# Eight raw first slots instead of seven, the eighth expert's weights read twice, and a new order

## The chip, the cores and the metric

The kernel runs on one core of a Trainium2 chip. The core has a matrix array (PE), a vector engine (DVE), an activation engine (ACT), GpSimd (POOL) and an engine that issues transfers (SP). ACT and GpSimd issue transfers too. The metric is the device time of one execution in microseconds. The time before is the median of three runs, 1015.27 us (1010.53 to 1015.96).

## The reference

A gated scan over 4 sequences of 5056 tokens with 256 features, and then a mixture of 8 experts of which each of the 20224 tokens takes the one with the highest logit:

```python
log_a = c * sig_r * np.log(np.clip(a_base, 1e-06, 1.0 - 1e-06))[None, None, :]
a_t = np.exp(log_a)
norm = np.sqrt(np.maximum(1.0 - a_t * a_t, 1e-06))
x_gated = norm * sig_i * x
for t in range(S):
    h = a_t[:, t] * h + x_gated[:, t]
    y[:, t] = h
...
logits = x @ w_gate                  # x is y, tokens by 256
e_idx = np.argmax(logits, axis=1)    # and gate_w, its softmax weight
eom = 1.0 / (1.0 + np.exp(-(x @ w_output_gate)))
for e in range(E):
    mask = e_idx == e
    h = np.maximum(x[mask] @ w1[e], 0.0)     # 256 x 1024
    ye = h @ w2[e]                           # 1024 x 256
    out[mask] = gate_w[mask, None] * eom[mask, e, None] * ye
```

Here sig_r, sig_i and a_base are sigmoids of r_gate, i_gate and a_param, and c is 8.

## The kernel before

**Chunks.** The 158 tiles of 128 tokens are taken in 21 chunks: two of 4 tiles, eighteen of 8, one of 6. A chunk's features lie on the partitions, in blocks of 512 tokens. For each chunk SP loads r, i and x (L659). ACT computes the gates by two tanh passes (L665, L668), the decay and its square by exponentials (L675, L679) and a square root (L684); the root and the exponential need different function tables, and each change of table is an instruction of its own. DVE forms the products (L671, L687) and scans along the tokens (L719). ACT and DVE then cut the state into a high and a low half precision part (L879, L886); between the parts lie 128 columns of zeros per tile, the pads, set by DVE at L884. A transposing DMA on SP's queue (L895) turns it into rows of tokens, and PE forms the logits (L903).

**Routing.** DVE finds each token's expert (`choose`, `chosen`), PE counts the token's rank among those of the same expert with a matmul against a triangle and, for each tile, one against ones (`ranks`, L960 and L962, nine matmuls for eight tiles), DVE turns the ranks to positions, the scale and the token's number (`weights`, L978 to L987). GpSimd writes each tile's rows to these positions in a store in DRAM (`xs`, L456, an indirect DMA).

**Slots.** A slot is up to 128 (later 256) rows of one expert. After the chunks 1, 3, 4, 5, 6, 8 and more, a set of eight slots follows, one for each expert (`SETS`): slots 0 to 7 belong to chunk 1, 8 to 15 to chunk 3, 16 to 23 to chunk 4. The last 19 and a loop for the rest choose their expert on the chip. A slot fetches its rows by a transposing DMA on SP (L1135), PE multiplies with w1 (tile ph), ACT takes the positive part (h, L1228 or L1232), DVE the low half of it (L1235), PE multiplies with w2 (po), ACT scales (ot, L1303), and GpSimd writes the rows to the output (L1306).

**Weights.** There are 16 units, w1 and w2 of each expert, 1 MB each. A unit is loaded in single precision (L512), PE forms a gram of it (pg, L538) from which a scale follows, and ACT (L580) and DVE (L590) cut it into two half precision parts. A split slot takes three products of such parts: 48 matmuls in layer 1 (L1207) and 24 in layer 2 (L1282). A plain slot multiplies with the raw weights in single precision (L1193, L1268), 16 matmuls in each layer, which the profile shows as 32 and 16 records. Plain are the slots 0 to 6. Expert 7's slot is split; its weights are staged in the ring `hh` (tiles fw). The raw unit u lies where the parts of unit u+2 will lie, so those can't be written until the slots that read the raw ones are done (`used_raw`).

**Order.** `in_order` (L120) is a planner written by hand: each piece of work has an engine, a cost, what it comes after, and a rank from tables (`UNIT_RANK`, `CHUNK_RANK`, `SLOT_RANK`, ...). It sets the order of PE, ACT and DVE. The DMA issues on SP and ACT's queue and GpSimd's work follow one another in the order in which the planner emits them (`queue`, L302). The load of unit u waits until that of unit u - 4 has landed (`DEPTH`). The store `xs` is first filled with rows of zeros, by two transfers (`fill`, tile zrow).

## Time and profile before

| | before |
|---|---|
| median of 3 runs | 1015.27 us |
| range | 1010.53 to 1015.96 us |
| profiled execution | 1015.02 us |
| its span | 1013.3 us |
| mean granted clock of PE | 0.986 |
| PE busy | 941.1 us (93%) |
| DVE busy | 681.7 us (67%) |
| ACT busy | 618.0 us (61%) |
| POOL busy | 345.6 us (34%) |

The span runs from the first to the last instruction; the profiled execution's time has 1.7 us around it. Busy times are unions over an engine's instructions. Times in views are counted from the start of the span. In a view an arrow with a name behind an instruction is what ended the idle time ahead of it.

### The profile page before, as it was taken

To read this page: it belongs to the slowest core of one execution; us is meant where nothing else is said; L and a number is where in the kernel's file an instruction comes from. 1 tells how busy PE (TensorE), PEld (TensorE's weight loads), DVE (VectorE), ACT (ScalarE), POOL (GpSimd) and SP (SyncE) were. 2 spreads that over 40 slices of the span, in tenths; PEclk is the share of its full clock that TensorE was granted. 3 is DMA by queue.
4 is the path that set the end of the run, shared out by engine and by line. 5 is a ranking of instruction groups with operands and counts; after the bars stand their busy time and mean duration, and the time that the engine had idled before them with its cause. 6 is when DMAs were issued, how large, how long until landed. Compare 5 with 4: busy or idle time off the path is not lost.

```text
span 1013.3 us, 27790 instructions
## 1 busy us (share of the span) xinstructions
PE 941.1 (93%) x10820; PEld 862.8 (85%) x10820; DVE 681.7 (67%) x1718; ACT 618.0 (61%) x929; POOL 345.6 (34%) x339
## 2 busy tenths in 40 slices
PE   1389958999999999999999999999999999999996
PEld 1279947999999899998888888888888888899996
DVE  5779999988988798888888888786222222222321
ACT  8779998886776777686768787732322223223332
POOL 1202353344445444444344434453211212121111
PEclk9989978999999999999999999999999999999999
DMA  9999678999999999999988798667212222137771
GB/s 332 388 315 236 175 226 213 217 195 204 216 248 192 241 213 234 189 226 224 226 208 218 198 233 218 141 132 222 58 53 53 53 54 44 46 110 250 225 229 44
DMA packets 269703, 189.96 MB, mean 187 GB/s; under 512 B 211548, under 2 KB 222558, under 8 KB 269568
## 3 DMA queue, kind: packets, MB, share of 16 engines
q1 hardware_dynamic: 249904, 138.57, 59.4%
q0 software_dynamic: 15456, 42.22, 13.2%
q10 hardware_dynamic: 4208, 7.34, 2.0%
q8 instruction: 88, 1.44, 0.6%
q14 instruction: 47, 0.39, 0.1%
HBM read 79.09 MB, written 45.02 MB: 122 GB/s over the span
## 4 chain that ended last, share of the span: by engine, by line
PE 64%; issue 13%; DMA 8%; DVE 6%; ACT 5%; POOL 3%; SPq 0%; POOLq 0%; ACTq 0%; DVEq 0%
PE ph L1207 29%; PE po L1282 28%; DMA xt<-xs 3%; DMA it<-in_i_gate_dram 2%; POOL out_dram L1306 2%; PE ph L1193 2%; DMA w1r<-in_moe_w_dram 2%; DMA rt<-in_r_gate_dram 1%; DVE h L1235 1%; PE lg L903 1%; DVE it L719 1%; PE pg L538 1%; PE po L1268 1%; DVE peak L771 1%; DMA out_dram<-ot,osc 1%
## 5 line engine op out<-in xcount | busy, mean ns | idle before, releaser
L1282 PE MATMUL po<-w2r,h 128*128 128x256 f16 (+1 forms) x3744 | 517.6, 273 | 3.7 <-DVE w2r L590 1.8
L1207 PE MATMUL ph<-xt,w1r 128*128 128x128 f16 (+1 forms) x4656 | 454.3, 242 | 10.0 <-DVE h L1235 3.2
L1207 PEld LDWEIGHTS <-w1r 128*128 128x128 f16 x4656 | 362.7, 98 | 40.0 <-issue 4.2
L1282 PEld LDWEIGHTS <-h 128*128 128x128 f16 x3744 | 346.1, 98 | 40.1 <-issue 5.7
L1235 DVE SCALAR_TENSOR_TENSOR h<-ph,h 128x512 f16<-128x512 f32 x312 | 206.4, 684 | 231.9 <-ACT h L1232 227.8
L1306 POOL DMA_INDIRECT out_dram<-ot,osc x163 | 167.8, 1030 | 397.9 <-ACT ot L1303 349.7
L1232 ACT ACTIVATE h<-ph 128x512 f16<-128x512 f32 x312 | 177.7, 592 | 193.8 <-PE po L1282 175.1
L456 POOL DMA_INDIRECT xs<-rows_all,posi x158 | 174.2, 1103 | 255.9 <-ACT h L1232 87.9
L1303 ACT ACTIVATE ot<-po,osc 128x256 f32<-128x256 f32 x163 | 72.3, 469 | 126.7 <-PE po L1282 63.6
L719 DVE TENSOR_TENSOR_SCAN it<-rt,last,it 128x512 f32<-128x512 f32 (+4 forms) x78 | 94.6, 1238 | 0.3
L1207 PE MATMUL ph<-xt,ws 128*128 128x128 f16 x912 | 69.5, 219 | 0.0
L1207 PEld LDWEIGHTS <-ws 128*128 128x128 f16 x912 | 60.5, 98 | 2.6
L687 DVE SCALAR_TENSOR_TENSOR it<-it,xt 128x1024 f32<-128x1024 f32 (+1 forms) x40 | 48.3, 1207 | 20.7 <-ACT it L684 20.7
L675 ACT ACTIVATE rt<-rt,lam 128x512 f32<-128x512 f32 (+1 forms) x80 | 61.2, 802 | 0.5
L886 DVE SCALAR_TENSOR_TENSOR rt<-it,scale,rt 128x512 f16<-128x512 f32 (+1 forms) x76 | 50.3, 702 | 11.8 <-ACT rt L879 11.5
L671 DVE SCALAR_TENSOR_TENSOR xt<-it,xt 128x1024 f32<-128x1024 f32 (+1 forms) x40 | 48.3, 1208 | 7.5 <-ACT it L668 7.4
L668 ACT ACTIVATE it<-it 128x1024 f32<-128x1024 f32 (+1 forms) x40 | 41.7, 1043 | 11.4 <-DMA it<-in_i_gate_dram 8.0
L665 ACT ACTIVATE rt<-rt 128x1024 f32<-128x1024 f32 (+1 forms) x40 | 41.8, 1044 | 10.0 <-DMA rt<-in_r_gate_dram 7.9
L679 ACT ACTIVATE it<-rt 128x1024 f32<-128x1024 f32 (+1 forms) x40 | 41.8, 1044 | 6.7 <-DVE xt L671 4.6
L684 ACT ACTIVATE it<-it,quarter 128x1024 f32<-128x1024 f32 (+1 forms) x40 | 45.1, 1135 | 0.3
L879 ACT ACTIVATE rt<-it,scale 128x1024 f16<-128x1024 f32 (+1 forms) x38 | 41.1, 1131 | 5.8 <-DVE scale L793 5.7
L771 DVE TENSOR_REDUCE peak<-it 128x1 f32<-128x1024 f32 (+1 forms) x34 | 39.5, 1195 | 0.0
(181 smaller groups left out, 674.3 us busy)
## 6 DMA issues: line engine op xcount, KB each, us to landing
rt<-in_r_gate_dram SPq DMA_DIRECT2D x39, 512.0 KB
it<-in_i_gate_dram SPq DMA_DIRECT2D x39, 512.0 KB
xt<-in_x_dram SPq DMA_DIRECT2D x39, 512.0 KB
ws<-w1r SPq DMA_DIRECT2D x38, 512.0 KB
w1r<-in_moe_w_dram ACTq DMA_DIRECT2D x4, 1024.0 KB
w2r<-in_moe_w_dram SPq DMA_DIRECT2D x4, 1024.0 KB
w2r<-in_moe_w_dram ACTq DMA_DIRECT2D x3, 1024.0 KB
w1r<-in_moe_w_dram SPq DMA_DIRECT2D x3, 1024.0 KB
```

Source lines behind the costliest of these rows:

```text
L456: op = nc.gpsimd.indirect_dma_start(out=xs[:, :], out_offset=bass.IndirectOffsetOnAxis(ap=pos, axis=0), in_=rows.bitcast(F32), in_offset=None,
L671: nc.vector.scalar_tensor_tensor(t("xt"), t("it"), 1.0, t("xt"), op0=ALU.add, op1=ALU.mult)
L675: nc.scalar.activation(r[:, h], r[:, h], AF.Exp, scale=lam[:, h:h + 1], bias=lam[:, h:h + 1])
L719: nc.vector.tensor_tensor_scan(H[:, h, lo:hi], A[:, h, lo:hi], H[:, h, lo:hi], first, op0=ALU.mult, op1=ALU.add)
L771: nc.vector.tensor_reduce(tiles["peak", c][:, b // 4:b // 4 + 1], tiles["it", key][:, :, 0:m], axis=AX.XY, op=ALU.max, apply_absolute_valu ...
L886: nc.vector.scalar_tensor_tensor(halves(key, 1, m // P)[:, :, h], of_tiles(key, m)[:, :, h], tiles["scale_of", c], halves(key, 0, m // P)[ ...
L1207: nc.tensor.matmul(ph[:, i, 0:w], lhsT=ws[:, f // 2 % 2, a, c, f % 2 * P:(f % 2 + 1) * P], rhs=xt[:, b * ND + c, 0:w], start=k == 0, stop= ...
L1232: newest["relu"] = nc.scalar.activation(part(0, f0), tiles["ph", s, f0][:, :, 0:w], AF.Relu).ins
L1235: nc.vector.scalar_tensor_tensor(part(1, f0), tiles["ph", s, f0][:, :, 0:w], 0.0, part(0, f0), op0=ALU.max, op1=ALU.subtract)
L1282: nc.tensor.matmul(po[0:pw, j], lhsT=hh[:, a, f % 4, j * P:j * P + pw], rhs=second(b), start=f + j + a + b == 0, stop=f == NF - 1 and a == ...
L1303: nc.scalar.activation(ot[0:pw], tiles["po", s][0:pw, j], AF.Copy, scale=tiles["osc", s][0:pw, j, 0:1])
L1306: op = nc.gpsimd.indirect_dma_start(out=out[:, :], out_offset=bass.IndirectOffsetOnAxis(ap=tiles["osc", s][0:pw, j, 1:2].bitcast(I32), axi ...
```

## The change

Expert 7 becomes the first in turn, and its raw weights take the places of expert 0's parts (`at = (u + 2) % 16`). All eight first slots are plain, and so are the second slots of experts 5 and 6 (`AGAIN`, slots 13 and 14). So expert 7's parts are cut later, from a second load in the ring `hh`, ahead of slot 19 (`RETURN`), and slot 15, its second one, follows slot 18. The logarithm in the decay, an activation before, is now a series on DVE alone. The pads are set by GpSimd, in its queue, and wait for the block's scan; the transposing DMA waits for them. GpSimd writes the tokens' numbers too. From chunk 8 on (`SUMS`) the ranks take three matmuls and a short scan on DVE in place of nine matmuls. Sums take one reduction for two, the weights one step fewer, and the last state is copied only at a chunk's end. The tables of ranks are new.

The diff, cut to its core:

```diff
-UNIT_RANK = (120.607, 156.984, -22.135, ...
+UNIT_RANK = (209.083, 164.775, 223.789, ...
-RAWS = 7
-LAST = 7
+AGAIN = (5, 6)
+RETURN = 19
+SUMS = 8
...
+    def size_of():
+        nc.vector.scalar_tensor_tensor(ab_, ap, -1.0, ap, op0=ALU.mult, op1=ALU.min)
+        nc.vector.tensor_scalar(lo, ap, 0.0, None, op0=ALU.min)
     def exp_of():
-        nc.scalar.activation(ab_, ap, AF.Exp, scale=-1.0)
+        nc.scalar.activation(ab_, ab_, AF.Exp)
-    def ln_of():
-        nc.scalar.activation(lo, ab_, AF.Ln)
...
-    def unit(u, staged):
+    def load_unit(u):
+        at = (u + 2) % len(units)
+        fw = place_of(at).bitcast(F32)
...
+            if at >= DEPTH:
+                tc.add_manual_dep(
+                    ins.ins, tiles["load", at - DEPTH].name,
...
+    def split_unit(u, staged=None):
...
+            read.append(work("SP", DMA_ISSUE, load, [old], UNIT_LOAD[u + 2], dma=2.6 / g, uses=[use], share=0.5 if i else 2.0))
...
+        def pads(key, m):
+            a = plane(key, 2, 0, 0)
+            queue("Pool", nc.gpsimd.memset(bass.AP(a.tensor, a.offset, [a.ap[0], [PITCH, m // P - 1], [1, P]]), 0.0))
         def rest_of(key, m):
-            if m > P:
-                a = plane(key, 2, 0, 0)
-                nc.vector.memset(bass.AP(a.tensor, a.offset, [a.ap[0], [PITCH, m // P - 1], [1, P]]), 0.0)
...
+                pw = [work("Pool", 0.4, lambda key=key, m=m: pads(key, m), [states[b // 4]], late_rank, uses=[pl])] if m > P else []
-                    work("SP", 0.85 + 1.45 * scale, lambda b=b, key=key, m=m: flip(b, key, m), [hw, lw] + olds, ...
+                    work("SP", 0.85 + 1.45 * scale, lambda b=b, key=key, m=m: flip(b, key, m), [hw, lw] + pw + olds, ...
...
+            if c >= SUMS:
+                up = tiles["up", c][:, 0:E * nt].rearrange("p (e j) -> p j e", e=E)
+                to = pk[:, 0:nt * E].rearrange("p (j e) -> p j e", e=E)
+                nc.tensor.matmul(to, lhsT=not_after, rhs=st("oh", E), start=True, stop=False, skip_group_check=True)
+                nc.tensor.matmul(to, lhsT=ones16, rhs=up, start=False, stop=False, skip_group_check=True)
+                nc.tensor.matmul(pk[:, nt * E:(nt + 1) * E], lhsT=ones16, rhs=up[:, nt - 1], start=False, stop=True, skip_group_check=True)
+                return
...
+        def numbers():
+            cuts = cuts_of(row_at, nt)
+            for b, e in zip(cuts[:-1], cuts[1:]):
+                mi = rows_all[:, row_at[b]:row_at[b] + e - b, META + 2:META + 4].bitcast(I32)
+                queue("Pool", nc.gpsimd.iota(mi, pattern=[[P, e - b], [0, 1]], base=(t0 + b) * P, channel_multiplier=1))
...
-        plain = expert is not None and c == min(SETS) and expert < RAWS
+        plain = expert is not None and (c == first_set or c == second_set and expert in AGAIN)
...
+    turn = [E - 1] + list(range(E - 1))
...
+        if c == first_set:
+            for e in turn[:AHEAD]:
                 weights_of(e)
+            for k, e in enumerate(turn):
+                if k + AHEAD < E:
+                    weights_of(turn[k + AHEAD])
+                slot(slots_in[c][e])
+            continue
         for s in slots_in[c]:
-            if s < n_full:
+            if s == RETURN:
+                for u in (2 * E - 2, 2 * E - 1):
+                    split_unit(u, STAGED[u])
+                slot(2 * E - 1)
+            if s < n_full and s != 2 * E - 1:
                 slot(s)
```

What moves stands in the order of the instructions. SP's queue, from the loads of the fourth chunk (names end in the chunk's number, its first tile and a serial number) to the first fetch; xt16_0 and xt16_7 are the rows of slot 0 and slot 7, xs the store, w1r and w2r the weights. Before:

```order
L659 DMA rt_3_4_282<-in_r_gate_dram 128x2x512
L512 DMA w2r_132<-in_moe_w2_dram 128x8x256
L512 DMA w1r_131<-in_moe_w1_dram 128x2x1024
L659 DMA it_3_0_363<-in_i_gate_dram 128x2x512
L512 DMA w2r_132<-in_moe_w2_dram 128x8x256
L659 DMA xt_3_4_451<-in_x_dram 128x2x512
L512 DMA w2r_132<-in_moe_w2_dram 128x8x256
L659 DMA xt_4_0_482<-in_x_dram 128x2x512
L512 DMA w1r_131<-in_moe_w1_dram 128x2x1024
L1124 TENSOR_LOAD firsti_1_416
L1135 ISA
L1135 DMA_TRANSPOSE xt16_0_567<-xs_84 128x4x128
```

After:

```order
L680 DMA rt_3_4_282<-in_r_gate_dram 128x2x512
L680 DMA it_2_4_309<-in_i_gate_dram 128x2x512
L504 DMA w1r_142<-in_moe_w1_dram 128x2x1024
L680 DMA it_3_0_408<-in_i_gate_dram 128x2x512
L504 DMA w2r_143<-in_moe_w2_dram 128x8x256
L504 DMA w1r_142<-in_moe_w1_dram 128x2x1024
L504 DMA w2r_143<-in_moe_w2_dram 128x8x256
L680 DMA xt_3_4_484<-in_x_dram 128x2x512
L680 DMA xt_4_0_512<-in_x_dram 128x2x512
L1178 TENSOR_LOAD firsti_1_469
L1189 ISA
L1189 DMA_TRANSPOSE xt16_7_517<-xs_84 128x4x128
```

The first fetch is one of expert 7 and follows loads of chunks 3 and 4; before, it followed a load of weights. The two fills of `xs` that stood apart (the second before chunk 11) are both issued ahead of the first fetch: the second stands one row ahead of the piece shown.

ACT's instructions where the split slots begin, up to the first relu of a split slot (h_7_0 before, h_8_0 after); dg is the square of a gram, ot a slot's result, fw14 the two staged halves of expert 7's w1, w1r and w2r the weights. Before:

```order
L544 ACTIVATE dg_14_1481,sq_14_1482<-pg_14_1455 128x128
L668 ACTIVATE it_5_0_1262<-it_5_0_1262 128x1024
L665 ACTIVATE rt_5_4_1389<-rt_5_4_1389 128x1024
L580 ACTIVATE w1r_131<-fw14_0_1401,wsc_133 128x4x256
L580 ACTIVATE w1r_131<-fw14_1_1421,wsc_133 128x4x256
L580 ACTIVATE w2r_132<-w2r_132,wsc_133 128x2048
L879 ACTIVATE rt_4_0_907<-it_4_0_741,scale_4_1499 128x4x256
L879 ACTIVATE rt_4_4_998<-it_4_4_1201,scale_4_1499 128x4x256
L675 ACTIVATE rt_5_0_1327<-rt_5_0_1327,lam_94 128x512 x2
L679 ACTIVATE it_5_0_1262<-rt_5_0_1327 128x1024
L1232 ACTIVATE h_7_0_1569<-ph_7_0_1512 128x4x128
```

After:

```order
L1357 ACTIVATE ot_3_0_1509<-po_3_1463,osc_3_1269 128x256
L1282 ACTIVATE h_6_1518<-ph_6_0_1372 128x512
L1282 ACTIVATE h_6_1518<-ph_6_4_1437 128x512
L598 ACTIVATE w1r_142<-w1r_142,wsc_144 128x4x256
L1357 ACTIVATE ot_4_0_1533<-po_4_1491,osc_4_1331 128x256
L598 ACTIVATE w1r_142<-w1r_142,wsc_144 128x4x256
L598 ACTIVATE w2r_143<-w2r_143,wsc_144 128x2048
L1357 ACTIVATE ot_5_0_1606<-po_5_1520,osc_5_1427 128x256
L1286 ACTIVATE h_8_0_1620<-ph_8_0_1567 128x4x128
L1286 ACTIVATE h_8_1_1666<-ph_8_4_1613 128x4x128
```

Before, the split slot 7 starts behind both staged halves of expert 7's w1, the split of a w2, two high parts of chunk 4 and chunk 5's decay. Now slot 8 is the first split slot; plain slots' relus and results and the splits of other experts' weights stand ahead of it, and no staged weights.

GpSimd's queue around the scatters of chunk 3 (posi_3). Before:

```order
L1306 DMA out_0_dram<-ot_4_0_1403,osc_4_1149 20224x256
L456 DMA xs_84<-rows_all_130,posi_3_1360 172032x264
L1306 DMA out_0_dram<-ot_5_0_1438,osc_5_1323 20224x256
L456 DMA xs_84<-rows_all_130,posi_3_1360 172032x264
L1306 DMA out_0_dram<-ot_6_0_1453,osc_6_1423 20224x256
L456 DMA xs_84<-rows_all_130,posi_3_1360 172032x264 x6
L456 DMA xs_84<-rows_all_130,posi_4_1729 172032x264
```

After:

```order
L921 MEMSET rt_4_0_979 128x3x128
L1042 IOTA rows_all_141 128x8
L461 DMA xs_84<-rows_all_141,posi_3_1213 172032x264 x5
L921 MEMSET rt_4_4_1016 128x3x128
L461 DMA xs_84<-rows_all_141,posi_3_1213 172032x264 x3
L1360 DMA out_0_dram<-ot_2_0_1381,osc_2_1112 20224x256
L1360 DMA out_0_dram<-ot_3_0_1509,osc_3_1269 20224x256
L1360 DMA out_0_dram<-ot_4_0_1533,osc_4_1331 20224x256
L1360 DMA out_0_dram<-ot_5_0_1606,osc_5_1427 20224x256
L1360 DMA out_0_dram<-ot_6_0_1749,osc_6_1633 20224x256
```

The pads of chunk 4's two blocks (rt_4_0, rt_4_4) and the row of numbers now stand ahead of and among the scatters of chunk 3.

## Rows read from the trace of the kernel before

**Rows 1.** The page, part 1: busy us, share of the span, instructions.

```profile
PE 941.1 (93%) x10820; PEld 862.8 (85%) x10820; DVE 681.7 (67%) x1718; ACT 618.0 (61%) x929; POOL 345.6 (34%) x339
```

**Rows 2.** Busy us by stretch: length, engines, PEclk, DMA share, GB/s.

```profile
0.00:71.80 71.80, 29.59 (x255) 26.59 (x255) 49.68 (x159) 54.64 (x76) 12.03 (x26) 0.95 1.04 356
71.80:131.90 60.10, 60.06 (x514) 55.69 (x515) 55.56 (x122) 57.62 (x79) 16.40 (x15) 1.00 0.86 213
131.90:162.00 30.10, 16.48 (x190) 13.00 (x189) 28.28 (x62) 29.48 (x36) 13.99 (x10) 0.72 0.72 188
162.00:300.00 138.00, 135.30 (x1941) 127.55 (x1939) 123.04 (x299) 107.57 (x154) 61.53 (x57) 1.00 0.99 218
```

**Rows 3.** Timeline of PE: start us, us, work, count [idle before <-releaser].

```profile
62.16 1.09 PE L538 MATMUL pg<-w1r 128*128 128x128 bf16 x16 [1.95 <-DMA w1r<-in_moe_w_dram]
...
71.77 2.50 PE L1193 MATMUL ph<-xt,w1r 128*128 128x128 f32 x20 [0.37 <-DVE xt L1177]
```

**Rows 4.** Timelines of ACT's and SP's DMA queues (ACTq, SPq).

```profile
52.11 0.39 ACTq L512 DMA_DIRECT2D w1r<-in_moe_w_dram  x1
...
62.13 0.39 SPq L512 DMA_DIRECT2D w1r<-in_moe_w_dram  x1
63.48 1.31 SPq L1135 DMA_TRANSPOSE xt<-xs  x1
```

**Rows 5.** Timeline of ACT: first plain relu, first relu of slot 8.

```profile
74.56 0.58 ACT L1228 ACTIVATE h<-ph 128x512 f32<-128x512 f32 x1
...
161.96 0.58 ACT L1232 ACTIVATE h<-ph 128x512 f16<-128x512 f32 x1
```

**Rows 6.** Groups of ACT, 74.5 to 162: count, busy us, mean ns, idle.

```profile
L580 ACT ACTIVATE w1r<-w1r,wsc 128x1024 f16<-128x1024 f32 x12 | 13.1, 1138 | 0.5 <-PE ph L1193 0.5
L580 ACT ACTIVATE w2r<-w2r,wsc 128x2048 f16<-128x2048 f32 x6 | 12.0, 1992 | 0.0
...
L684 ACT ACT_TABLE_LOAD x5 | 6.4, 1283 | 0.1
L668 ACT ACTIVATE it<-it 128x1024 f32<-128x1024 f32 x6 | 6.3, 1047 | 0.5 <-DMA it<-in_i_gate_dram 0.5
```

**Rows 7.** Chain that ended last, 0 to 330: start us, us, PE's pieces.

```profile
93.05 1.35 PE po L1268 x6
...
95.14 5.02 PE ph L1193 x44
...
205.48 1.97 PE po L1282 x18
...
265.41 1.68 PE ph L1207 x30
```

**Rows 8.** A group of PE, 71.7 to 162: rank matmuls.

```profile
L962 PE MATMUL pk<-oh,ones 128*128 128x64 f16 (+7 forms) x24 | 1.1, 187 | 0.0
```

**Rows 9.** Groups of DVE, 74.5 to 162: the lower halves of the splits.

```profile
L590 DVE SCALAR_TENSOR_TENSOR w1r<-w1r,wsc 128x1024 f16<-128x1024 f32 x12 | 15.0, 1279 | 0.3 <-ACT w1r L580 0.3
L590 DVE SCALAR_TENSOR_TENSOR w2r<-w2r,wsc 128x2048 f16<-128x2048 f32 x6 | 14.1, 2345 | 0.0
```

**Rows 10.** DMA issues by tile: xcount, KB each.

```profile
xs<-zrow SPq DMA_DIRECT2D x2, 1056.0 KB
```

**Rows 11.** DVE's pads and POOL's scatters over the span; one scatter.

```profile
L884 DVE MEMSET rt<- 128x192 uint32 x37 | 8.1, 218 | 0.0
...
L456 POOL DMA_INDIRECT xs<-rows_all,posi x158 | 174.2, 1103 | 255.9 <-ACT h L1232 87.9
...
147.56 2.51 POOL L456 DMA_INDIRECT xs<-rows_all,posi  x1 [2.57 <-ACT h L1232]
```

**Rows 12.** Waits of PE over the span: us in total, times, longest us.

```profile
PE prow L839 <- DVE last L722: 20.1, 1, 20.1
...
PE ph L1207 <- DVE h L1235: 3.2, 5, 1.0
...
PE ph L1207 <- DMA xt<-xs: 1.7, 3, 1.0
```

263 lines of the change are left out of this document (142 added, 121 removed).

## The prediction

> **What bounds the kernel now.** I read the page's first part, then busy time by stretch, and only then single waits. The page says that the array (PE) is busy 93% of the span [rows 1]. The stretches say that the missing 7% lie in two places at the front [rows 2]: to 71.8 us PE works 29.59 us, and from 131.9 to 162 us 16.48 of 30.10. Between them it is full (60.06 of 60.10), after them nearly (135.30 of 138, and no great gap later). So a microsecond is won where PE is idle in front, or where PE's work shrinks.
>
> The first gap ends with the first plain matmul at 71.77 [rows 3]. Ahead of it PE waits for the weights of unit 4, whose gram starts at 62.16; totals, logits and three more grams follow. The queue views tell why so late [rows 4]: ACT's queue issues unit 4 at 52.11 only, and SP, waiting for that transfer before its own weight load, issues this at 62.13 and the first fetch of routed rows (on the same queue) at 63.48.
>
> The second gap is ACT's. From the first plain relu at 74.56 to slot 8's first relu at 161.96 [rows 5] lie 87.4 us, and rows 2 show ACT busy 57.62 of 60.10 and 29.48 of 30.10 there: 96 to 98%. DVE is below that in the first of the two (55.56). PE is done with the seven plain slots at 131.9 and waits, since ACT (gates of the coming chunk, weight splits, table loads [rows 6]) hands over the split weights late. So that stretch lasts as long as ACT's list of work, and what leaves that list shortens it one for one, until DVE is as long.
>
> **The change part by part.**
>
> *Start (order).* The SP order now has the fetch for expert 7 right behind the loads, not behind a load that waits for unit 4. PE still needs a gram of the unit that ACT's queue issues last, so the landing at 62.2 stays; what follows it before the first plain matmul is one gram (1.1), totals (0.6), logits and another gram, 4 to 5 us where 9.6 lay [rows 3]. I take 67, against 71.8. Bounds: 62, if that unit's load leaves the queue earlier, and 72, if nothing moves. The order also puts the second fill of the routed store (xs<-zrow, 1056 KB [rows 10]) into the loads at the start: at the 356 GB/s of the first stretch [rows 2] that is 1.1 MB / 356 = 3.0 us of transfers, an upper bound, and inside those bounds. The logarithm's table load and the one back go, 2 x 1.28 = 2.6 us (a table load of rows 6), but ACT idles there for data later; I take 0, bounds 0 and -2.6. With the 2.8 us from first matmul to first relu as before (74.56 - 71.77), the first relu is at 69.8.
>
> *ACT's list from there to the first relu of slot 8.* By the order, and with the means of rows 6: two halves of w1 fewer (2 x 1.14 = 2.3), one w2 split fewer (2.0), two split pieces of the eighth expert's staged second weights moved behind (128x1024, as a half of w1: 2 x 1.14 = 2.3), five gate passes of 1024 columns moved behind (20 to 15, 5 x 1.05 = 5.2), table loads 9 to 5 (4 x 1.28 = 5.1), one result (0.5) and a small exponential (0.3). That is 17.7; back-to-back instructions overlap by some 0.1 us each, so 17. The eighth plain slot's two relus replace two of the split slot. So 87.4 - 17 = 70.4, and slot 8's relu comes at 69.8 + 70.4 = 140.2, not 161.96: **21.8 us earlier**. PE's work in that stretch, 8 plain slots of some 7.2 us and 9 us of grams, logits and ranks, is about 67 us, so PE and ACT are now nearly equal there and the gap of rows 2 is closed.
>
> *What PE still owes at that point, or owes more.* A plain slot is 32 layer-1 matmuls at 5.02/44 = 0.114 and 16 layer-2 ones at 1.35/6 = 0.225: 7.25 us. A split one is 48 at 1.68/30 = 0.056 and 24 at 1.97/18 = 0.109: 5.31 [rows 7]. So 1.9 us for each plain slot more. Slots 13 and 14 turn plain behind the point: 2 x 1.9 = 3.8. The order leaves 7/8 of slot 6's second layer behind slot 8's first relu: 14 x 0.225 = 3.1. Chunk 4's logits and ranks there: 0.7. In all 7.6 to pay. Ranks cost 6 matmuls fewer in 13 chunks, 78 of 64 columns at half the 0.056 of 128 columns, 2.2 us (1.1 us busy for 24, thus 0.046 each, gives 3.6 [rows 8]); I take 2.2. Net **-5.4**, so 21.8 becomes 16.4.
>
> *What is late next.* The work moved behind lands in the stretch of rows 2 that ended at 300: splits of three units' worth on ACT (10.6 us) and on DVE (12.2: 4 w1 halves of 1.279, three w2 of 2.345 [rows 9]) and put-off chunk work: on ACT the five passes (5), on DVE by the order a gated product, a peak, two scans, one chunk's routing of some 16 steps at about 0.2 and two lows of slot 15 (together about 9.7). ACT has 30 us free there (107.57 of 138), DVE only 15 (123.04 of 138). DVE gains some 4 us from chunk work (pads, below; row numbers; copies of the last state) and 2.7 from the two plain slots without a low part (4 x 0.68). So DVE comes out at 123 + 12.2 + 9.7 - 6.7 = 138 of 138, as full as PE. Where the order is not perfect, PE waits, most likely at slots 16 to 20, just before the second splits of expert 7. Bounds 0 (all fits) and 10 (half of it lies on the path); nearest are PE's present waits for DVE's low parts, 3.2 us in all [rows 12], and I take **4**. Sum: 1015.0 - 16.4 + 4 = 1002.6, **1003**. The profiled execution's 1015.02 is the median of the runs (1015.27) within 0.03%, so no correction.
>
> *Edits with one answer.* Pads leave DVE (37 x 218 ns = 8.1 us [rows 11]), row numbers too; DVE isn't the bound after 300, so 0 there, and in 162 to 300 it is in the 4 us above. If that cover is missing, it is part of the 0 to 10. The 2 MB loaded twice replace the 2 MB staged before, beside the once loaded: 2 MB more at 213 GB/s, hidden, since PE worked 60.06 of 60.10 us there beside 213 GB/s [rows 2]; if they aren't, 10 us, the upper bound of what comes back.
>
> **Pads on GpSimd, the edit that can cost.** A pad waits for its block's scan, and stands in GpSimd's queue among the scatters and results; behind it wait the scatters (PE's later fetches need them) and the transposing DMA. In the trace scatters take 1.10 us on the mean, but one takes 2.51 at 147.56 [rows 11], when DVE was in a weight split, 2.345 each [rows 9]. PE waited for fetched rows just 1.7 us in three places [rows 12], so there is slack; I take 0, bounds 0 and 42 (below). The Trainium skill (SBUF — State Buffer, "SBUF: two separate sides") says that DVE and GpSimd share a port pair as an exclusive lock and that the loser blocks for the whole instruction. It speaks against this edit; the stretched scatter agrees with it, a shared bandwidth would also look like this, and no run here separates the two.
>
> **The rivals.**
> *A, hardly a change.* The start stays at 71.8 (nothing gained of the 4.8) and the moved work comes back in full (10, not 4): 1003 + 4.8 + 6 = **1014**. For it: unit 4's load at 52.11 is not moved forward; DVE would be as full as PE. Against: the ACT sum doesn't depend on either. Also in this class: the change doesn't close the gap because DVE, not ACT, sets the stretch (DVE 28.28 of 30.10 in the gap [rows 2]); then 87.4 falls not to 70.4 but to some 78, and the time is 1011.
> *B, slower.* GpSimd's queue. One place, every chunk from 4 on (17): a pad stands ahead of scatters of the former chunk and waits for a scan. Each may hold the queue by a scan or a DVE instruction, up to the 2.51 of rows 11: 17 x 2.51 = 42, 1045. It decides from (1020.4 - 1003)/17 = 1.0 us lost by PE per chunk; 1.5 would give **1028**. For it: the order, and the stretched scatters. Against: POOL is busy 34% [rows 1], and rows are fetched well ahead [rows 12].
> *C, the first instruction.* PE's first is now the gram of unit 14, whose load ACT issues behind its first tanh (about 6.5 us). Unit 4 took 10.05 from issue to gram [rows 3, 4]: 16.5; the first projections wait until 20.1 anyway [rows 12]. Even at 22 it costs 2 us of a start that the loads bound: 1003 to **1005**, part of the forecast.
> *D, better.* The start comes at 62 and nothing comes back: 1003 - 5 - 4 = **994**.
>
> **How the numbers follow.** Forecast with C (997 to 1010) 0.58, D (below 997) 0.14, A (1010 to 1020) 0.17, B (above) 0.11. A measurement here can tell about 0.5% from no change, 1010.2 to 1020.4. So faster 0.72, same 0.17, slower 0.11. The range 991 to 1015 leaves out some 0.05 below and 0.15 above.
>
> **What would show it.** Right: first plain matmul near 67; from the first plain relu to slot 8's first relu about 70 us (87.4) with ACT over 95% busy; no PE gap like that of 131.9 to 162; PE's waits between slots 8 and 20 some 4 us, ended by DVE; PE's busy total up by 3.5 (5.7 for three more plain slots less 2.2). Wrong: PE waiting for xt<-xs or for flips in chunk after chunk (B); a stretch of 78 us or more with DVE full (A); waits of 10 us around slots 13 to 20 (A); a first plain matmul behind 72.

## The result

The changed kernel takes **1019.87 us** (median of 6 runs, 1019.34 to 1021.25), the kernel before beside it 1011.62 (1009.47 to 1015.96): a ratio of **1.0076**, interval 1.006 to 1.0092. It is slower by three quarters of a per cent, where 1003 was forecast, and 1019.87 lies outside the range of 991 to 1015. In the profiled executions the span goes from 1013.3 to 1017.5: only 4.2 us, since the profiled one of before (1015.02) is at the slow end of its six runs. So the traces show about half of the 8.3 us between the medians.

The page's first part of after, against [rows 1] (busy us, share of the span, instructions):

```profile
PE 948.9 (93%) x10672; PEld 871.5 (86%) x10672; DVE 673.5 (66%) x1606; ACT 608.3 (60%) x920; POOL 389.9 (38%) x405
```

ACT and DVE have less to do, as the diff says; PE has 7.8 us more in 148 fewer instructions. Where the time went is read from busy time by stretch, cut here at first relus: of the first plain slot, of slot 8, of slot 14, of slot 20 and of slot 32 (length, then busy us of PE, PEld, DVE, ACT, POOL, then PE's granted clock, DMA share, GB/s). After:

```profile
0.00:73.48 73.48, 31.82 (x272) 29.37 (x273) 48.04 (x155) 46.92 (x71) 13.13 (x31) 0.74 1.04 358
73.48:148.62 75.14, 69.70 (x615) 64.59 (x614) 61.77 (x132) 67.78 (x92) 32.05 (x29) 0.98 0.83 216
148.62:183.80 35.18, 35.18 (x447) 33.33 (x443) 33.80 (x73) 28.75 (x38) 17.14 (x16) 1.00 0.82 200
183.80:237.00 53.20, 41.83 (x482) 36.79 (x481) 40.52 (x91) 38.70 (x51) 20.86 (x21) 0.87 0.91 217
237.00:302.95 65.95, 65.95 (x948) 62.66 (x946) 59.37 (x134) 52.32 (x76) 35.34 (x34) 1.00 0.97 210
302.95:1017.50 714.55, 704.39 (x7925) 644.73 (x7922) 430.05 (x1027) 373.86 (x597) 271.42 (x278) 1.00 0.68 164
```

The same cut of before:

```profile
0.00:74.56 74.56, 32.35 (x279) 29.35 (x280) 51.03 (x161) 57.37 (x80) 12.03 (x26) 0.95 1.06 346
74.56:161.96 87.40, 73.73 (x680) 65.89 (x679) 82.45 (x182) 84.33 (x109) 30.35 (x24) 0.90 0.79 208
161.96:195.10 33.14, 31.46 (x460) 29.68 (x457) 30.39 (x73) 28.14 (x40) 13.10 (x13) 1.00 0.99 226
195.10:227.60 32.50, 32.13 (x462) 30.16 (x461) 28.18 (x75) 25.18 (x38) 17.00 (x14) 1.00 0.98 203
227.60:295.75 68.15, 67.50 (x964) 63.66 (x961) 60.33 (x146) 50.05 (x73) 31.29 (x29) 1.00 0.98 220
295.75:1013.30 717.55, 703.96 (x7993) 644.12 (x7990) 429.34 (x1088) 372.90 (x595) 241.79 (x234) 1.00 0.67 163
```

Read down the lengths: 1.1 us won to the first relu, 12.3 to slot 8's, 2.0 lost to slot 14's, then **20.7 lost between slots 14 and 20** (53.20 against 32.50), 2.2 won to slot 32's and 3.0 behind it. The one stretch turns a gain of 11.3 into a loss of 9.4. (The same six slots lie in it before and after; slot 15 has only changed its place.) In it PE is busy 41.83 of 53.20, at a mean clock of 0.87, where before it was busy 32.13 of 32.50. DVE (40.52) and ACT (38.70) are not full either.

What PE waits for there, in after (us in total, times, longest):

```profile
PE lg L821 <- DVE dp L817: 3.1, 1, 3.1
PE ph L1261 <- ACT w1r L598: 2.8, 2, 1.7
PE po L1322 <- ACT ot L1357: 2.4, 1, 2.4
PE ph L1261 <- DVE w1r L608: 1.9, 2, 0.9
PE po L1336 <- DVE h L1289: 1.0, 1, 1.0
```

Five different partners: the peaks of chunk 6 (dp), the second split of expert 7 (w1r), the ring of two result buffers (ot), and a hidden activation (h). And the clock falls where PE pauses. The two stretches at 0.50 of it (1.2 of the 2.4 GHz) that cost most, in the same columns as above; PE had been busy 1.87 of the 5 us ahead of the second:

```profile
29.10:66.60 37.50, 18.06 (x138) 16.72 (x139) 24.30 (x75) 22.58 (x37) 9.45 (x12) 0.50 1.09 388
...
216.80:227.10 10.30, 5.53 (x62) 4.52 (x62) 7.77 (x13) 7.64 (x8) 7.02 (x7) 0.50 0.89 298
```

Together with 3.40 us from 192.9 on, 8.9 us of PE's work between slots 14 and 20 ran at half clock; half of that, some 4.5 us, is my estimate of the loss. So the 20.7 are about 11.0 of idle time (11.37 against 0.37), 4.5 of clock, and 5 of more work in the stretch (the plain slots 13 and 14 for the most part, and 12 logits and a set of ranks that before stood elsewhere).

### The profile page after: what moved, and what is told of

Read it like the earlier page. It is cut to its first block, busy times and chain, and to the rows that moved or that the text cites. A ratio compares the mean times of both kernels' runs of the same rounds, so it can differ in the third digit from the quotient of the medians.

```text
span 1017.5 us, 27514 instructions
## 1 busy us (share of the span) xinstructions
PE 948.9 (93%) x10672; PEld 871.5 (86%) x10672; DVE 673.5 (66%) x1606; ACT 608.3 (60%) x920; POOL 389.9 (38%) x405
## 4 chain that ended last, share of the span: by engine, by line
PE 64%; issue 12%; ACT 7%; DVE 6%; DMA 5%; POOL 3%; SPq 1%; ACTq 0%; POOLq 0%; DVEq 0%
PE ph L1261 30%; PE po L1336 28%; POOL out_dram L1360 2%; PE po L1322 2%; PE ph L1247 2%; DMA w1r<-in_moe_w_dram 1%; DMA it<-in_i_gate_dram 1%; DVE h L1289 1%; SPq L934 1%; PE lg L942 1%; ACT rt L696 1%; DMA out_dram<-ot,osc 1%; POOL xs L461 1%; ACT it L700 1%; DVE it L744 1%
## 5 line engine op out<-in xcount | busy, mean ns | idle before, releaser
L1336 PE MATMUL po<-w2r,h 128*128 128x256 f16 (+1 forms) x3672 | 480.7, 272 | 1.2 <-DVE h L1289 1.2
L1261 PE MATMUL ph<-xt,w1r 128*128 128x128 f16 (+1 forms) x4512 | 422.6, 242 | 5.8 <-ACT w1r L598 2.8
L1261 PEld LDWEIGHTS <-w1r 128*128 128x128 f16 x4512 | 347.6, 98 | 36.2 <-ACT w1r L598 6.6
L1289 DVE SCALAR_TENSOR_TENSOR h<-ph,h 128x512 f16<-128x512 f32 x306 | 202.7, 684 | 237.4 <-ACT h L1286 233.2
L1360 POOL DMA_INDIRECT out_dram<-ot,osc x163 | 184.7, 1133 | 414.2 <-ACT ot L1357 372.9
L461 POOL DMA_INDIRECT xs<-rows_all,posi x158 | 182.1, 1152 | 169.2 <-ACT h L1286 49.6
L1261 PE MATMUL ph<-xt,ws 128*128 128x128 f16 x912 | 65.0, 219 | 0.0
L744 DVE TENSOR_TENSOR_SCAN it<-rt,last,it 128x512 f32<-128x512 f32 x40 | 50.7, 1275 | 0.2
L700 ACT ACTIVATE it<-rt 128x1024 f32<-128x1024 f32 (+1 forms) x40 | 41.6, 1043 | 10.6 <-DVE xt L692 10.0
L744 DVE TENSOR_TENSOR_SCAN it<-rt,it,it 128x512 f32<-128x512 f32 (+4 forms) x38 | 45.2, 1204 | 0.2
L1247 PE MATMUL ph<-xt,w1r 128*128 128x128 f32 x320 | 43.5, 287 | 0.7 <-ACT h L1282 0.5
```

The source lines that it names most:

```text
L461: op = nc.gpsimd.indirect_dma_start(out=xs[:, :], out_offset=bass.IndirectOffsetOnAxis(ap=pos, axis=0), in_=rows.bitcast(F32), in_offset=None,
L700: nc.scalar.activation(t("it"), t("rt"), AF.Square)
L744: nc.vector.tensor_tensor_scan(H[:, h, lo:hi], A[:, h, lo:hi], H[:, h, lo:hi], first, op0=ALU.mult, op1=ALU.add)
L1247: nc.tensor.matmul(ph[:, i, 0:w], lhsT=raw[2 * expert][:, c * F + f * P:][:, 0:P], rhs=tiles["x32", s][:, c], start=c == 0, stop=c == ND - 1,)
L1261: nc.tensor.matmul(ph[:, i, 0:w], lhsT=ws[:, f // 2 % 2, a, c, f % 2 * P:(f % 2 + 1) * P], rhs=xt[:, b * ND + c, 0:w], start=k == 0, stop= ...
L1289: nc.vector.scalar_tensor_tensor(part(1, f0), tiles["ph", s, f0][:, :, 0:w], 0.0, part(0, f0), op0=ALU.max, op1=ALU.subtract)
```

## The experiments

Each run was timed beside the kernel before on the same chip. The chips differ: before takes 1012 to 1014 us on those of the first, third and fifth group, 1032 on those of the second and fourth; so ratios to before of the same chip are compared, and of the traces the stretch from slot 14 to 20 ("stretch" below, first relu to first relu), in which the chips agree within 2 us. The changed kernel itself was not timed on the slower chips: there the nearest to it is the run that moves four instructions of chunk 7 (1.0072). The first theory was rival B (GpSimd's queue) against "moved work comes back" (A).

**First group: one suspect at a time.**

Pads and row numbers back on DVE; the other engines' order stays as in after:

```
-  queue("Pool", nc.gpsimd.memset(<pads of a block>, 0.0))
-  queue("Pool", nc.gpsimd.iota(mi, ...))
+  nc.vector.memset(<pads of a block>, 0.0)
+  nc.vector.tensor_scalar(<row numbers>, ids[:, b:e], float(t0 * P), None, op0=ALU.add)
```

> The changed kernel, with the pads and the tokens' numbers set by DVE again (same order of PE, ACT and SP; GpSimd has 74 instructions fewer). Theory Q (GpSimd's queue: pads and numbers hold up scatters, results and the transposing DMA): the waits of PE between slots 14 and 20, 8.7 us more than before, go for the greater part, 1010 to 1014 us. Theory R (the second load of expert 7's weights and its place set those waits): 1018 to 1022 us, the waits at 209 to 223 us as in the changed kernel, since DVE gets some 12 us more and GpSimd was not late.

1020.59, ratio 1.0075 (1.006 to 1.0089): no difference to after. The ot wait goes, the others stay, and a fetch takes its place; slot 20 comes at 237.4 instead of 237.0. PE's waits, 186 to 240:

```profile
PE ph L1266 <- ACT w1r L598: 3.4, 2, 2.1
PE lg L821 <- DVE dp L817: 3.1, 1, 3.1
PE ph L1266 <- DVE w1r L608: 1.9, 2, 1.0
PE ph L1266 <- DMA xt<-xs: 1.6, 1, 1.6
PE po L1341 <- DVE h L1294: 1.0, 1, 1.0
```

Rival B falls, as far as pads and numbers go.

The second fill of the routed store, which in after leaves SP at 23.3 us, held back behind the loads issued before it, as in the kernel before (one SP row moves):

> The changed kernel, with the second fill of the routed store held behind the loads of chunk 11 again, where it was before (nothing else moves). If its 1.06 MB among the first loads is what kept the start late: first plain matmul 3 us earlier, at 68 (70.9), and 1016 to 1018 us. If it is the clock or the order of the loads: first plain matmul within 1 us, 1019 to 1021 us.

1020.9, ratio 1.0088 (1.0068 to 1.0107), first relu at 74.4 (after 73.5): the fill costs nothing at the start.

A third result buffer (`tag="ot", bufs=3`), against ACT's wait for a store that landed 8.6 us behind its issue:

> The changed kernel with a third buffer for the results (ot), in the same order; the buffer's space comes from a constant that no chunk uses. ACT waited 2.8 us for a result's store at 191 us, and PE 2.4 us for ACT, after which the granted clock was at half for 3.4 us. If that wait is on the path: slot 16 about 4 us earlier (195), 1015 to 1017 us. If slot 15 waits for expert 7's second load anyway: slot 16 earlier, slot 20 where it is (237), 1019 to 1021 us.

1020.82, ratio 1.0072 (1.0055 to 1.0089). The ot wait is gone and slot 16 comes 11.4 us behind slot 14 instead of 15.1; but slot 20 comes at 238.5, no earlier, and PE waits 3.9 us for ACT's second split, in after 2.8. (After run once more, below, has 4.0 there without the third buffer, so that growth by itself says nothing.) What slot 16 gains is gone by slot 20.

`RETURN = 23` instead of 19, so that slot 15 and the second load of expert 7 come four slots later (planned anew):

> The changed kernel with the second split of expert 7 (and slot 15) ahead of slot 23 instead of 19; the planner lays the order anew from there. Theory R (the second load and split of expert 7 come before ACT, DVE and the DMA have room): the wait of some 9 us at 209 to 223 goes or halves, 1010 to 1015 us. Theory A (DVE and ACT have as much to do as PE there, whatever the place): the waits come somewhere else between slots 14 and 24, 1017 to 1022 us.

1031.66, ratio 1.019 (1.017 to 1.021). Slots 19 to 21 do come earlier (21 at 226.8 instead of 241.9): from slot 14 to 20, now without slot 15 in it, PE is busy 32.1 of 35.8 us, and it takes chunk 6's spread of peaks at 222.82 without a wait. Then slot 22 to 23 takes 32 us. PE's longest waits, 186 to 290:

```profile
PE lg L821 <- DVE dp L817: 8.5, 1, 8.5
PE po L1336 <- ACT h L1286: 4.2, 1, 4.2
PE po L1322 <- ACT ot L1357: 3.7, 1, 3.7
```

The 8.5 us for dp are now those of the next chunk, at 256.15. In this run the hole has moved to where slot 15 and a chunk's peaks meet again, and is larger.

**Second group: the split, the chunk, the clock, the ranks.**

No second load and split of expert 7 (DVE clears in their place):

> The changed kernel without the second load and the second split of expert 7's weights (its parts are set to zero by DVE in their place, so the rows of expert 7 from slot 15 on come out wrong; all other work stands, in the same order). Theory R (the 2 MB load, 4.5 us of ACT and the wait for them at slot 15 are the lost time): of the 9 us of waits at 209 to 224 two thirds go, 1012 to 1015 us. Theory C (the sixth chunk's chain of gates, scan and peak is late, and slot 15 stands behind its matmul in PE's order): the 3.1 us wait for the peak stays, the others shrink by 3 us, 1015 to 1018 us.

1032.06, ratio 1.0001 (0.9982 to 1.002). On this chip all that was lost seemed to be back, though the stretch is 49.8 us long in the profiled execution (which at 1038.28 is 6 us above the median). The third group repeats it. Here, and in all runs that leave splits out, the later weights of those experts are zero. That zeros make PE itself faster shows in no trace: from slot 32 to slot 120 the runs with zeros take 701.0 to 704.5 us on the slower chips, those without 701.7 to 704.9.

Four instructions of chunk 7 on ACT moved behind chunk 6's root:

> The changed kernel with ACT's tanh, two exponentials and square of chunk 7's first block put behind the square root of chunk 6's second block (four instructions moved, nothing else). Theory C (ACT waits in its order for chunk 7's load and so delays chunk 6's scan, peak and the matmul that slot 15 stands behind): the peak some 4 us earlier, the 3.1 us wait of PE gone, 1015 to 1018 us. Theory R (slot 15 waits for the second load of expert 7): that wait is then longer by as much, 1019 to 1021 us.

1040.18, ratio 1.0072 (1.0045 to 1.01): nothing; the root comes no earlier (212.3; in after 209.3, with slot 14 4.0 us earlier too), as ACT then waits in its own order for PE's slots.

40 and 80 idle matmuls ahead of the second and third gram, to keep the clock up at the start:

> The changed kernel with 40 and 80 needless small matmuls on PE ahead of the second and the third gram, where PE waits for loads. The granted clock was at half from 29 to 67 us; the grams of that time took 1.9 us, not 1.08. If the half clock is what keeps the first plain matmul at 70.9: full clock in that stretch, the matmul 3 to 6 us earlier, and 1015 to 1018 us if the lead lasts, 1019 to 1021 if it is given back between slots 14 and 20. If the loads keep it there: within 1 us of 70.9.

1036.03, ratio 1.005 (1.0028 to 1.0072). The mean clock of the first 74 us rises from 0.74 to 0.82, and the first relu is at 74.6. This doesn't tell loads from clock: PE still waits 17.5 us for loads of w1, but the grams at 56.92, 63.44 and 65.52 also still take 1.87 to 1.91 us, so the clock was not kept up where they stand. Any gain is within the error of the comparison.

The kernel **before** with the new ranks (a scan on DVE and three matmuls) from chunk 8 on:

> The kernel before, with one part of the change alone: from chunk 8 on the ranks by three matmuls and a scan on DVE (78 matmuls of PE fewer, 13 scans of 64 columns on DVE more, everything else in its old order). By the prediction's term 2.2 us less (3.6 at most): 1009 to 1011 us against 1012 to 1013. If DVE's scan delays the ranks as much as PE gains: no difference.

1031.82, ratio 0.9998 (0.9978 to 1.0018): within some 2 us of nothing; the predicted 2.2 lies at the very edge of this.

**Third group: again, and two together.** The changed kernel once more gave 1020.91, ratio 1.0082 (1.0061 to 1.0103), stretch 51.4 with PE busy 39.3, so 1.7 us less than the first time with nothing changed:

> The changed kernel once more, on the chip of the three that follow, since two earlier sets of runs were on chips of unequal speed: 1.006 to 1.009 of the kernel before, slot 20 some 38 us behind slot 16.

No second split once more:

> As before: the changed kernel without the second load and split of expert 7's weights (zeros in their place, so expert 7's rows from slot 15 on are wrong; the order of all else is kept). Theory R (the second split alone): 0.999 to 1.002 of the kernel before, and slot 20 at most 32 us behind slot 16. Theory B (chunk 6's chain and the second split, each in front of slot 15): about 3 us off, 1.003 to 1.006, slot 20 some 35 us behind slot 16.

1019.88, ratio 1.0061 (1.004 to 1.0082), stretch 52.5. So the split is worth some 0.2% here, which the two intervals don't tell from nothing, and the 0.7% of the second group (against 1.0072 on that chip) was not repeated; why it was larger there stays open.

Chunk 6's second block (gate, gated product, square, root, scans, peaks, level, high) brought forward by hand among ACT's and DVE's slots:

> The changed kernel with chunk 6's second block brought forward on ACT and DVE (gate, square and root ahead of slot 14's second relu, scan and peak among the lows of slots 16 and 17, level and high and low parts ahead of expert 7's second split; some 12 instructions of ACT and 21 of DVE change place, nothing on PE). Theory B: PE's 3.1 us wait for the peak goes, but slot 15 then waits for the second split, which no one moved: at most 2 us off, 1.005 to 1.009. Theory C (chunk 6's chain alone): 1.000 to 1.003.

1023.97, ratio 1.0106 (1.0091 to 1.0121). The wait for dp is gone, as meant. In its place, 184 to 241:

```profile
PE ph L1268 <- ACT w1r L598: 6.3, 2, 4.0
PE po L1330 <- ACT ot L1365: 4.1, 1, 4.1
PE ph L1268 <- DVE w1r L608: 2.6, 2, 1.6
PE po L1344 <- DVE h L1296: 1.5, 1, 1.5
```

Both together:

> Both edits of the two runs ahead together (without the second load and split, zeros in their place; chunk 6's second block early). Theory B: nothing is left in front of slot 15, the 9 us of waits at 209 to 224 go as a whole: slot 20 some 29 us behind slot 16, 0.997 to 1.000 of the kernel before, more than the sum of the two apart. If a third thing holds slot 15: as without the second split alone.

1020.47, ratio 1.0068 (1.0052 to 1.0084), stretch 49.3: 2 to 4 us less than the two runs of after. All of after's larger waits are gone or smaller, and new ones stand there (h 2.5, rt 2.0 and 1.6).

**Fourth group: three, and four, together.** No second split, chunk 6 early and the third buffer:

> The changed kernel with the three single edits together: no second load and split of expert 7 (its second weights are zero, so the rows of that expert in later slots are wrong), chunk 6's second block brought forward on ACT and DVE, and a third buffer for results. The one-wait theory: the waits between slots 14 and 20 stand behind one another, so with all three gone the 14 us that lie there above PE's own work come back, about 1007 against 1020 of the changed kernel, ratio near 0.995. The theory that PE has run ahead of the chunk line and the put-off splits: a fourth wait comes up and the time is 1017 to 1021, ratio 1.004 to 1.008.

1037.51, ratio 1.0046 (1.0026 to 1.0066), stretch 52.6. The one-wait theory in its strong form falls: 1007 was its forecast.

Second slots of experts 5 and 6 split again (`AGAIN = ()`, planned anew):

> The changed kernel with the second slots of experts 5 and 6 split as before (first slots of all eight stay in single precision), so their weights must be split before slot 13, and the planner sets the order anew from the same table. If plain slots 13 and 14 and the splits put off behind them are the cause, PE's own work falls by 3.8 and the 12 us come back: about 1008. If not, PE meets the same waits earlier: 1016 to 1025, with about 20 us of idle time between the last first slot and slot 24.

1052.6, ratio 1.0188 (1.0155 to 1.0221). Slot 12 is at 180.7 instead of 170.9, and the 14-to-20 stretch is 61.5 us all the same, with PE waiting 6.9 us for a choice of experts and 3.3 and 3.1 for chunk 6. So there is a hole without plain slots 13 and 14 too. The orders differ in too much to say more.

No splits of experts 5, 6 and 7 at all:

```
   def hi(k=k):
+      if staged or u in (10, 11, 12, 13):
+          return
   def lo(k=k):
+      if staged or u in (10, 11, 12, 13):
+          nc.vector.memset(<this part of the place>, 0.0)
+          return
```

> The changed kernel with the splits of experts 5, 6 and 7 left out (their later weights are zero; the rows of these experts in later slots are wrong; a clear on DVE stands where each low half was). That takes some 13 us off ACT and 10 off DVE in the stretch of slots 8 to 24. If put-off splits are what PE meets there: slots 14 to 20 take about 40 us, not 53, and the time is 1007 to 1011, ratio 0.994 to 0.998. If the chunk line alone is what PE meets: 50 us there as in the other runs, 1017 to 1020, ratio 1.004 to 1.007.

1032.89, ratio 1.0007 (0.9988 to 1.0026), stretch 52.5, ACT busy 33.1 in it instead of 38.7. The ratio lies where no second split alone lay on a chip of the same kind (1.0001): taking the other splits too brings nothing more, and the stretch is as long as in after. **It is not the amount of put-off split work on ACT**, which from slot 8 to slot 32 is busy 110.3 us instead of 119.8. DVE's share was hardly tested: it has clears where the low parts stood, and is busy 130.6 instead of 133.7. And the profiled execution (1038.61) is the slowest of twelve, so what the median of 1032.89 won, no trace shows.

All four:

> The two together: no splits of experts 5, 6 and 7 (zero weights, as in the run without late splits), chunk 6's second block brought forward and a third buffer for results. All causes named so far for the stretch from slot 14 to 20 are gone then, so the theory that PE has run ahead of this work has it PE-bound, about 37 us, and the time near 1004 to 1007. If it stays above 1014, the cause lies elsewhere: in PE's own list or the clock.

1034.13, ratio 1.0026 (1.0005 to 1.0046). This is the telling run: the waits named first (ot, dp, the second split) are gone, and the stretch is still 52.2 us, PE busy 42.07 of it, DVE 38.5, ACT 32.9. Its line, and what ACT and PE wait for in turn (timelines: start, us, work, [idle before <-releaser]):

```profile
186.70:238.90 52.20, 42.06 (x482) 37.54 (x479) 38.48 (x92) 32.88 (x44) 17.56 (x21) 0.87 0.86 198
```

```profile
215.73 1.06 ACT L694 ACTIVATE rt<-rt 128x1024 f32<-128x1024 f32 x1 [3.68 <-DMA rt<-in_r_gate_dram]
...
218.46 2.17 ACT L930 ACTIVATE rt<-it,scale 128x1024 f16<-128x1024 f32 x2
```

```profile
211.09 0.29 DVE L829 TENSOR_SCALAR dp<-iw,peak 128x128 bf16<-128x128 f32 x1
...
215.40 0.22 PE L833 MATMUL lg<-dp,ones_b 128*128 128x128 bf16 x1
...
219.65 0.22 PE L955 MATMUL lg<-g,rt 128*128 128x48 bf16 x2 [3.03 <-ACT rt L930]
```

PE waits for chunk 6's high plane (L930), which stands on ACT behind the first gate of chunk 7's second block (L694), which waits for a load. It has a second cause, in PE itself: the high plane needs the spread of the peaks (L833), and PE gets to this 4.0 us after dp is written (211.38), with no idle time just ahead of it, since slot 18's second layer stands before it in PE's order. Why is the load late? The same loads and flips on SP's queue, after:

```profile
182.81 5.27 SPq L934 DMA_TRANSPOSE rows_all<-rt  x1
...
196.94 0.39 SPq L680 DMA_DIRECT2D rt<-in_r_gate_dram  x1
...
197.94 5.41 SPq L934 DMA_TRANSPOSE rows_all<-rt  x1
...
208.87 0.39 SPq L680 DMA_DIRECT2D rt<-in_r_gate_dram  x1
```

and before:

```profile
182.76 4.25 SPq L895 DMA_TRANSPOSE rows_all<-rt  x1
...
187.82 4.04 SPq L895 DMA_TRANSPOSE rows_all<-rt  x1
...
194.32 1.13 SPq L659 DMA_DIRECT2D rt<-in_r_gate_dram  x1
...
198.53 0.46 SPq L659 DMA_DIRECT2D rt<-in_r_gate_dram  x1
```

Chunk 5's first flip leaves at the same time, the second 10 us later, and the load that takes its buffer 10 us later. In after's order three fetches of slots stand between the flips and two more ahead of the load, and fetches wait for PE to free their buffers (9.0 us in six waits from 150 to 260; in before, too, 10.0 in eight). That gave a last theory, SP's order.

**Fifth group: SP's order.** Chunk 5's second flip and chunk 7's loads ahead of the fetches of slots 17, 18, 15 and 19; on the other engines nothing moves:

```
+  for anchor, moved in (
+      (("fetch", 16), [("flip", (5, 4)), ("lr", (7, 0)), ("lx", (7, 4))]),
+      (("fetch", 17), [("lr", (7, 4))]),
+  ):  # each group is moved to just behind its anchor
```

With all four edits:

> The run of all four edits (no splits of experts 5 to 7, their weights zero; third result buffer; chunk 6's second block early), and on SP's queue the second flip of chunk 5 and chunk 7's loads ahead of the fetches of slots 17, 18, 15 and 19 instead of behind them; nothing moves on the other engines. Theory of SP's order: in the run of all four, ACT still waited 3.7 us at 215.7 for chunk 7's load, which SP issued at 211.8 behind fetches that wait for the array to free their buffers, and chunk 6's high plane stands behind that on ACT and its logits behind that on PE. Then that load leaves by 203, ACT's wait and PE's 3.0 for it go, slots 14 to 20 take 46 us or less instead of 52.2, ratio 0.996 to 1.000. Theory that the chunk line is late for itself: slots 14 to 20 stay at 50 to 53 and the ratio at 1.001 to 1.004.

1019.33, ratio 1.0065 (1.0049 to 1.0082). Alone:

> The changed kernel with only that edit on SP's queue: the second flip of chunk 5 and chunk 7's loads ahead of the fetches of slots 17, 18, 15 and 19. If SP's order alone holds the array: ACT's wait of 2.1 for the load goes, slots 14 to 20 take 45 to 49 us, ratio 1.001 to 1.004. If the waits stand behind one another, as in all single edits: slots 14 to 20 stay at 50 to 54, since PE's wait of 3.1 for the peaks of chunk 6 and its waits for expert 7's second split are there as before, ratio 1.006 to 1.009.

1022.99, ratio 1.0105 (1.0084 to 1.0126), stretch 52.6. In both the load leaves at 199 to 201 and ACT no longer waits for it. In the first, chunk 6's high plane begins at 220.2 nonetheless (all four: 218.5): now slot 17's rows come late, and PE takes the spread at 218.26, 6.0 us after dp. Its PE timeline, and its line for the stretch:

```profile
202.45 3.38 PE L1279 MATMUL ph<-xt,w1r 128*128 128x128 f16 x30 [5.38 <-DMA xt<-xs]
```

```profile
184.30:235.50 51.20, 41.78 (x481) 38.04 (x478) 38.64 (x91) 33.18 (x44) 17.52 (x21) 0.87 0.81 181
```

The 10 us by which the load is earlier are paid with 5.4 us of a fetch. SP's order by itself is not the cause either, but one more link.

**What the runs say together** (stretch is from slot 14's to slot 20's first relu; * marks the chips on which before takes 1032 us, and on which the changed kernel itself was not timed):

```
                               stretch  PE busy  ratio
before                           32.5    32.1    1
after                            53.1    41.8    1.0076
after once more                  51.4    39.3    1.0082
 pads and numbers on DVE         51.3    39.8    1.0075
 third result buffer             51.8    40.3    1.0072
 RETURN = 23 (no slot 15 in it)  35.8    32.1    1.019
 no second split (2nd group)     49.8    41.7    1.0001 *
 no second split (3rd group)     52.5    43.5    1.0061
 chunk 6 early                   55.9    40.6    1.0106
 both of these                   49.3    39.6    1.0068
 and the third buffer            52.6    40.6    1.0046 *
 second slots split              61.5    41.7    1.0188 *
 no late splits                  52.5    43.3    1.0007 *
 all four                        52.2    42.1    1.0026 *
 all four, and SP's order        51.3    41.9    1.0065
 SP's order alone                52.6    41.7    1.0105
```

In all orders that keep slot 15 behind slot 18 and were not planned anew, 49 to 56 us remain, whatever is taken away; PE idles 8 to 15 of them, and the mean clock in them is 0.84 to 0.93. Shown is that none of the larger waits that the trace of after names (dp, ot, the second split) is the cause by itself, nor the three or four edits together, nor the amount of split work on ACT. Nor is it the load on the DMA engines: in the stretch their share is 0.98 before and 0.91 after, and without the second load of expert 7 it falls to 0.79 to 0.86 while the stretch stays.

Argued, not shown, is what is left: the order on PE itself, against a chunk that is late. In before, and in after:

```profile
204.57 0.29 DVE L780 TENSOR_SCALAR dp<-iw,peak 128x128 bf16<-128x128 f32 x1
...
205.26 0.22 PE L784 MATMUL lg<-dp,ones_b 128*128 128x128 bf16 x1
```

```profile
216.75 0.24 PE L821 MATMUL lg<-dp,ones_b 128*128 128x128 bf16 x1 [3.13 <-DVE dp L817]
```

In after PE has chunk 6's spread of peaks (216.75) and its logits (from 224.13) behind slot 18, about slot 15's first layer; in before the spread is at 205.26 and the logits at 211.1 to 213.8, about slots 16 and 17. The slots come 9 to 10 us earlier than before up to there (18 at 207.4, before 216.8), but the chunk comes later: its root on ACT is at 209.3 instead of 191.6, and its dp is written at 216.70 instead of 204.86, 11.8 us later. So PE reaches the chunk's steps early and waits. And bringing the chunk forward by hand didn't bring it back to its old time: with all four edits dp is there at 211.38, still 6.5 us later than in before, and then PE takes the spread only at 215.40. In all five runs with chunk 6 early the spread waits 4 to 6 us for its turn on PE; so there PE's order holds back the very chunk for which PE then waits. RETURN = 23, where the spread stands behind slot 20's first relu and isn't waited for, fits this too. Moving the spread ahead of slot 18's second layer in the run of all four, or spread and logits behind slots 15 and 19 in after, would test it; neither was tried. No version beat the kernel before.

## Why the prediction was wrong

**Start: 67 was too early.** First plain matmul at 70.86, first relu at 73.48 (69.8 predicted): 3.7 of the miss. The step taken was that the last gram lands at 62.2 and only 4 to 5 us follow. PE's timeline of after:

```profile
54.57 1.89 PE L531 MATMUL pg<-w1r 128*128 128x128 bf16 x16 [9.78 <-DMA w1r<-in_moe_w_dram]
...
69.74 1.08 PE L531 MATMUL pg<-w2r 128*128 128x128 bf16 x16 [0.71 <-DVE wsq L544]
...
70.86 0.69 PE L1247 MATMUL ph<-xt,w1r 128*128 128x128 f32 x4
```

The load that PE waits for lands at 54.6 now, 7.6 earlier than in [rows 3]; but its gram, five more, totals and logits follow, at half clock up to 66.6 (1.89 instead of 1.08 each). I had counted two grams. The upper bound of 72 held; its reason was not thought of.

**ACT's list: right; "one for one": only until PE was the bound.** ACT is busy 67.78 from first relu to slot 8's, 16.5 less than the 84.33 of before, 17 predicted. The stretch is 75.14, not 70.4, because PE is busy 69.70 of it (I had 67 and wrote "nearly equal") and waits 3.3 us for the squares of gram diagonals on ACT and 1.3 for DVE. 4.7 of the miss. With two engines equally full and handing work to each other, the stretch is longer than either. Slot 8's relu comes 13.3 earlier instead of 21.8.

The next two terms are read from slot 8's to slot 32's first relu, after and then before (columns as above):

```profile
148.62:302.95 154.33, 142.96 (x1870) 132.78 (x1867) 133.69 (x296) 119.78 (x162) 73.34 (x69) 0.96 0.92 210
161.96:295.75 133.79, 131.09 (x1879) 123.49 (x1876) 118.90 (x291) 103.36 (x148) 61.39 (x56) 1.00 0.98 217
```

**What PE owes: right.** PE is busy 142.96 against 131.09: 11.9 more, of which some 4.5 are the clock, so 7.4, against 7.6 predicted.

**What comes back: the failed step.** I took 4 with bounds of 0 and 10, from sums of the work that was moved here. The sums came out: DVE is busy 14.8 us more (12.2 + 9.7 - 6.7 = 15.2 predicted), ACT 16.4 more (10.6 + 5 = 15.6). What failed is the step from how full an engine is to how long PE waits for it: "all fits" was to cost nothing, and the waits were sized by PE's old ones. In fact DVE is busy 133.69 of 154.33 us and ACT 119.78, neither is full, and PE idles 11.4 us all the same, against 2.7 before, waiting for single instructions of theirs; and the clock takes 4.5 more: 8.7 + 4.5 = 13.2 where 4 stood. That is 9.2 of the miss, and the bound of 10 was too narrow as well: it had no term for the clock, though [rows 2] show 0.72 in the gap of before. The place was right (slots 16 to 20, just before expert 7's second split), the mechanism was not: of the 11.2 us of waits shown above DVE ended 6.0 and ACT 5.2. Which order of instructions makes them is the part that stays open.

**Ranks.** Behind slot 32 the kernel gains 3.0, of which 2.2 were put on the ranks; the run that changed the ranks alone saw 0 within 2 us, so this isn't confirmed.

Sum: 3.7 + 4.7 + 9.2 - 0.2 (7.4 instead of 7.6) - 0.8 (3.0 instead of 2.2) + 0.1 (what lies around the span) = 16.7, the distance from 1002.6 to the 1019.34 of the profiled execution. That it closes is no proof, since the lengths of stretches always add up. And it starts from 1015.0, which was taken for the kernel before; six runs give 1011.62, so between the medians some 4 us more were missed (12.4 won were forecast, 8.3 were lost), and no trace here shows them.

**The rivals.** A named the right kind of ending (PE waits between slots 13 and 20 for what was moved behind), was within 1 us on the start (71.8; 70.86) and had the nearest time, 1014; it lacked PE as the bound of the first stretch (4.7) and the clock. B named the right sign with the wrong mechanism: no PE wait ends on a pad, and the first run puts pads and numbers back without effect. The Trainium skill (SBUF — State Buffer, "SBUF: two separate sides") has the shared pair of ports locked for a DVE instruction in a 2-port mode, or for one with two inputs in SBUF only against a GpSimd instruction that reads SBUF. A pad only writes, so the section says less against this edit than the prediction took from it. Here a pad took 0.44 us on GpSimd against 0.22 on DVE, which doesn't tell a lock from a slower engine, and ratios of 1.0075 with pads on DVE and 1.0076 and 1.0082 without show no cost to the kernel. C: PE's first gram ran at 14.03 (16.5 forecast) and its first projections at 22.26 instead of 20.14; whether these 2 us reach the first relu no run shows. D didn't come.

**The chances.** 0.72 for faster rested on the first stretch, where the work that leaves is easy to add up. Where that work and PE's lead land had two bounds, but no row of before that showed such a landing; this should have stood for more than 0.28.

## What to carry to other kernels

A gap that is closed in front moves the bounding engine ahead of everything behind it; before counting the gain, follow the in-order queues (here ACT, DVE, SP, GpSimd's and PE's own) to the first place where a chain that did not get faster must hand over, and price the gain only up to there. If the planner's other chains (a chunk's gates, scans and peaks) keep their old times, or come later as here, the lead is lost there, plus what the clock takes during the pause. That the engines' work fits into a stretch doesn't tell that it comes in time. In such a place removing single waits returned nothing here: take several away together in one run, and if the stretch keeps its length, look at the order of the waiting engine itself. And run the unchanged kernel once more: its stretch moved by 1.7 us, as much as most edits did.
